# Fewer VectorE instructions and 640 side columns on DMA engines 0 to 4, in a decode layer with attention and a gated feed-forward

## The chip, the cores and the metric

The kernel runs on one core of a Trainium2 chip. The time of a run is device microseconds of that core. The span, which the profile shows, goes from the core's first to its last instruction and is about 2 us shorter than the time.

Names: PE is TensorE, DVE is VectorE, ACT is ScalarE, POOL is GpSimd, SP is SyncE. "DMA engine n" is one of the core's 16 DMA engines. A DMA over 128 rows (SBUF partitions) makes 128 packets in these traces and ends with 16 increments, so each DMA engine is taken to carry 8 rows. A completion increment is the step of a DMA's semaphore when one of its DMA engines has delivered its share. What waits for the load waits for the last increment (w1 before: last increment at 98.76 us, PE starts on it at 98.80). A traced instruction is one that the profile records, the waits included.

## The reference, cut to what matters

```python
# B = 4, D = 1024, Hq = 32, Hkv = 4, Dh = 128, F = 3584; one new token, the last 2048 cached keys
q = layernorm(x) @ wq                                  # wq: 1024 x 4096
o = softmax(q k^T / sqrt(128)) v                       # k, v: 4 batches x 4 heads x 2048 x 128
h = x + o @ wo                                         # wo: 4096 x 1024
n = layernorm(h)
out = h + (silu(n @ w1) * (n @ w3)) @ w2               # w1, w3: 1024 x 3584, w2: 3584 x 1024
```

All of it is bf16. The core reads 55.6 MB of weights and cache for four tokens.

## The kernel before

One SyncE queue streams the weights and the cache through a ring in SBUF, in a fixed order; each load waits only until its place in the ring is free.

```python
    CE = 512
    SETS = [(0, 5, 4), (80, 3, 4)]               # first row, DMA engines, tiles

    def load_side(r0, ne, ns):                   # some rows of wq's last CE columns
        t = ktpool.tile([P, JG * QD * 16], BF16, tag="kT")
        rows = A_wq[r0 * KC : (r0 + ne * 4 * ns) * KC, N_Q - CE : N_Q]
        rows = rows.rearrange("(t i k) n -> k i t n", i=ne, k=KC)[KC - 1]
        nc.sync.dma_start(out=t[: ne * 4, : ns * CE], in_=rows)
        return [t[: ne * 4, k * CE : (k + 1) * CE] for k in range(ns)]

    def load_tail(at, src, n, r0, m):            # the other half of wq, without those columns
        t = ring[:, at : at + m * n]
        nc.sync.dma_start(out=t[:, : m * n - CE], in_=src[:, r0 * n : (r0 + m) * n - CE])
        # ... cut
    plan = [
        ("wq", load_rows, (0, wq_v, N_Q, 0, 4)),
        ("side", load_side, SETS[0]),
        ("side", load_side, SETS[1]),
        ("wq", load_tail, (32 * KIB, wq_v, N_Q, 4, 4)),
        # ... k, v, wo, w1, w3 (cut)
        ("w2", load_rows, (56 * KIB, w2_v, D, 0, 17)),
        ("w2", load_rows, (90 * KIB, w2_v, D, 17, 7)),
        ("w2", load_rows, (104 * KIB, w2_v, D, 24, 3)),
        ("w2", load_rows, (110 * KIB, w2_v, D, 27, 1)),
    ]
```

The side loads are a balancing trick. Each of the 128 rows of wq's second half is loaded without its last 512 columns, which takes 8 KB off every DMA engine. These 128 pieces come in two extra DMAs shaped so that only a few DMA engines serve them: 80 pieces on DMA engines 0 to 4 (16 each) and 48 on 0 to 2 (16 each). PE multiplies them apart.

K is transposed by PE in 16 units of 16 blocks; each unit's result is copied from PSUM half by DVE and half by ACT, and the scores of a unit follow one unit later.

```python
    for u, (b, n) in enumerate(units):
        # ... k_v and kT (cut)
        for t in range(NJ // TB):                          # two halves of 8 blocks
            kt_ps = psA.tile([P, TB, P], BF16, tag=f"kt{nt % 4}")
            # ... 8 transposes (cut)
            if nt % 2 == 0:
                nc.vector.tensor_copy(out=kT[:, t * TB : (t + 1) * TB, :], in_=kt_ps[:])
            else:
                nc.scalar.copy(out=kT[:, t * TB : (t + 1) * TB, :], in_=kt_ps[:])
            nt += 1
        if u >= 1:
            emit_scores(u - 1)
        # ... cut
```

## Time and profile before

| | before |
|---|---|
| time, median (range) | 137.80 us (137.72 to 137.94, 6 runs) |
| span of the profiled run | 136.0 us |
| busy: PE, DVE, ACT, POOL | 72.3, 43.9, 31.0, 1.7 us |
| moved | 55.75 MB, mean 410 GB/s |
| w1 issued, landed | 76.27, 98.76 us |
| last w2 load landed | 132.68 us |

These lines are from the page of the kernel before: busy time by engine, the DMA share in 40 slices (tenths), what was moved, the DMA queues (packets, MB, share of 16 engines' span), and the chain of work that ended last, by engine.

```profile
span 136.0 us, 2436 instructions
...
PE 72.3 (53%) x1096; PEld 46.1 (34%) x1096; DVE 43.9 (32%) x79; ACT 31.0 (23%) x36; POOL 1.7 (1%) x8
...
DMA  5999999999999999999989999989989899999970
...
DMA packets 2650, 55.75 MB, mean 410 GB/s; under 512 B 296, under 2 KB 464, under 8 KB 720
...
q1 hardware_dynamic: 2604, 55.58, 95.6%
q8 instruction: 8, 0.13, 0.3%
...
q14 instruction: 2, 0.02, 0.0%
...
DMA 54%; PE 25%; ACT 11%; DVE 5%; SPq 2%; issue 1%; ACTq 0%
```

DMA stands at 8 or 9 tenths almost throughout, while no compute engine is over 53% busy. Two queues carry instructions: q8 brought eight packets, q14 two. They look negligible, at 0.3% and 0.0%.

The chain in order of time (start, us, what) shows that most of its last 60 us is waiting for landings; "ring<-in_B_w_dram" is the loads of w1, w3 and w2, L459 the w1 matmuls, L514 the last cast.

```profile
74.79 1.46 PE OT_ps L382 x48
...
76.27 22.49 DMA ring<-in_B_w_dram
...
98.80 1.68 PE g_ps L459 x14
100.48 29.74 DMA ring<-in_B_w_dram
...
133.08 0.27 ACT res L514
```

The two groups of DVE instructions that the change touches most (busy us and mean ns after the first bar, idle time before them after the second), and two waits (us in total, times, longest):

```profile
L323 DVE COPY kT<-kt_ps 128x1024 bf16<-128x1024 bf16 x16 | 11.1, 692 | 16.5 <-PE kt_ps L319 16.5
...
L356 DVE TENSOR_SCALAR z<-pt_ps,mask 128x512 bf16<-128x512 f32 x8 | 5.5, 741 | 1.2 <-ACT z L360 0.8 <-PE pt_ps L352 0.3
```

```profile
PE g_ps L459 <- DMA ring<-in_B_w_dram: 4.9, 1, 4.9
...
PE scores_ps L304 <- ACT kT L325: 2.9, 7, 0.6
```

PE waits 4.9 us for w1. This is the slack of the compute work between w1's issue and its landing. The issue of w1 has a slack of its own: the queue is still busy with wo, whose increments come from 80.02 to 81.87 us.

The single packets, read from the trace's record of them, give the time that one packet takes on its DMA engine:

```
bytes            512   1024   1280   2048   16384   31744   32768   57344   65536
median us      0.027  0.046  0.055  0.084   0.611   1.175   1.215   2.116   2.418
(1280: from the kernel after; 8 ns and about 27 GB/s fit all of them)
```

These are the 16 completion increments of the last w2 load (one row of w2 per partition), in us:

```
before  130.94 131.20 131.37 131.56 | 132.24 132.30 132.43 132.49 132.53 132.54 132.57 132.57 132.58 132.63 132.63 132.68
```

Four DMA engines are done about 1.2 us before the other twelve. What follows the last one is short; the timeline's last rows (start, us, engine, line, what) are the last matmul, the cast and the store:

```profile
132.79 0.23 PE L492 MATMUL yb_ps<-ring,hgT 128*32 128x128 bf16 x4
...
133.08 0.27 ACT L514 CAST res<-yb_ps 128x128 bf16<-128x128 f32 x1 [26.10 <-PE yb_ps L492]
133.39 0.64 ACTq L515 DMA_DIRECT2D out_dram<-res  x1
```

### The profile page before, as it was taken

How to read it: one execution, taken by the hardware profiler on the slowest of the kernel's cores; microseconds unless marked ns; L12 is line 12 of the kernel's file. 1: busy time of each engine (PE TensorE's matmuls, PEld its weight loads, DVE VectorE, ACT ScalarE, POOL GpSimd, SP SyncE). 2: the span in 40 equal slices, each digit the busy share in tenths (PEclk: the TensorE clock that was granted, in tenths of full speed). 3: DMA queues.
4: the chain of work that ended last, by engine and by line, in shares of the span. 5: the costliest groups of instructions: out<-in, count | busy, mean ns of one | idle time of the engine just before them, and what ended most of it. 6: DMA issues, size and time to landing. Idle time of an engine off the chain costs nothing.

```text
span 136.0 us, 2436 instructions
## 1 busy us (share of the span) xinstructions
PE 72.3 (53%) x1096; PEld 46.1 (34%) x1096; DVE 43.9 (32%) x79; ACT 31.0 (23%) x36; POOL 1.7 (1%) x8
## 2 busy tenths in 40 slices
PE   0004920979898989810525916791097000970981
PEld 0002300268374756500014905570043000430870
DVE  5055000043344444470994001206200596026010
ACT  3000000015555555609294300000001400000000
POOL 5000000000000000000000000000000000000000
PEclk9999975557999999985555555568556855568568
DMA  5999999999999999999989999989989899999970
GB/s 155 464 463 406 412 420 414 429 424 439 424 439 424 424 443 426 410 552 453 463 347 463 463 410 405 477 354 494 439 371 494 371 472 401 399 420 407 424 298 5
DMA packets 2650, 55.75 MB, mean 410 GB/s; under 512 B 296, under 2 KB 464, under 8 KB 720
## 3 DMA queue, kind: packets, MB, share of 16 engines
q1 hardware_dynamic: 2604, 55.58, 95.6%
q8 instruction: 8, 0.13, 0.3%
q10 hardware_dynamic: 36, 0.02, 0.0%
q14 instruction: 2, 0.02, 0.0%
HBM read 55.59 MB, written 0.01 MB: 409 GB/s over the span
## 4 chain that ended last, share of the span: by engine, by line
DMA 54%; PE 25%; ACT 11%; DVE 5%; SPq 2%; issue 1%; ACTq 0%
DMA ring<-in_B_w_dram 38%; DMA ring<-in_A_wq_dram 15%; PE kt_ps L319 11%; ACT kT L325 5%; PE scores_ps L304 5%; ACT z L360 3%; PE q_ps L263 3%; DVE rmax L336 2%; ACT Pm L341 2%; PE OT_ps L382 2%; DVE pT L350 1%; SPq L120 1%; PE g_ps L459 1%; DVE z L356 1%; ACT L341 1%
## 5 line engine op out<-in xcount | busy, mean ns | idle before, releaser
L325 ACT COPY kT<-kt_ps 128x1024 bf16<-128x1024 bf16 x16 | 15.9, 1013 | 13.4 <-PE kt_ps L319 13.4
L319 PE MATMUL kt_ps<-ident,ring 128*128 128x128 bf16 x256 | 18.0, 232 | 0.0
L319 PEld LDWEIGHTS <-ring 128*128 128x128 bf16 x256 | 16.0, 105 | 4.9 <-issue 4.9
L323 DVE COPY kT<-kt_ps 128x1024 bf16<-128x1024 bf16 x16 | 11.1, 692 | 16.5 <-PE kt_ps L319 16.5
L459 PEld LDWEIGHTS <-hnT 128*32 128x32 bf16 x128 | 5.5, 143 | 21.8 <-issue 19.2
L382 PE MATMUL OT_ps<-z,ring 128*128 128x32 bf16 x256 | 7.5, 188 | 8.5 <-ACT z L360 5.0
L459 PE MATMUL u_ps<-ring,hnT 128*32 128x448 bf16 x64 | 6.0, 563 | 11.0 <-DMA ring<-in_B_w_dram 11.0
L304 PE MATMUL scores_ps<-kT,qz 128*32 128x512 bf16 x64 | 9.9, 609 | 2.9 <-ACT kT L325 2.9
L263 PE MATMUL q_ps<-ring,xnT 128*4 128x512 bf16 x63 | 6.7, 595 | 7.8 <-DMA ring<-in_A_wq_dram 7.8
L382 PEld LDWEIGHTS <-ring 128*128 128x128 bf16 x256 | 7.4, 104 | 9.2 <-issue 9.2
L459 PE MATMUL g_ps<-ring,hnT 128*32 128x448 bf16 x64 | 5.9, 558 | 4.9 <-DMA ring<-in_B_w_dram 4.9
L492 PEld LDWEIGHTS <-hgT 128*32 128x32 bf16 x156 | 4.9, 134 | 6.2 <-issue 5.7
L411 PE MATMUL y_ps<-ring,o 128*32 128x256 bf16 x128 | 5.9, 371 | 0.8 <-DVE o L398 0.8
L514 ACT CAST res<-yb_ps 128x128 bf16<-128x128 f32 x1 | 0.3, 266 | 26.1 <-PE yb_ps L492 26.1
L492 PE MATMUL y_ps<-ring,hgT 128*32 128x256 bf16 x68 | 3.8, 419 | 4.4 <-DMA ring<-in_B_w_dram 4.4
L360 ACT ACTIVATE z<-pt_ps,mask 128x512 bf16<-128x512 f32 x8 | 5.3, 687 | 3.5 <-DVE z L356 3.5
L352 PE MATMUL pt_ps<-pT,perm 128*128 128x512 bf16 x4 | 2.4, 607 | 6.8 <-DVE pT L350 6.8
L263 PEld LDWEIGHTS <-xnT 128*4 128x4 bf16 x63 | 2.0, 115 | 11.7 <-issue 11.6
L194 PE MATMUL tp_ps<-ident,xn 4*128 4x4 bf16 x8 | 0.7, 200 | 10.0 <-DVE xn L187 10.0
L356 DVE TENSOR_SCALAR z<-pt_ps,mask 128x512 bf16<-128x512 f32 x8 | 5.5, 741 | 1.2 <-ACT z L360 0.8
L473 DVE RECIPROCAL eg<-eg 128x896 f32<-128x896 f32 x1 | 5.8, 5753 | 0.0
L411 PEld LDWEIGHTS <-o 128*32 128x32 bf16 x128 | 4.4, 131 | 3.1 <-DVE o L398 1.9
(85 smaller groups left out, 50.1 us busy)
## 6 DMA issues: line engine op xcount, KB each, us to landing
ring<-in_B_w_dram SPq DMA_DIRECT2D x2, 7168.0 KB, 22.5
ring<-in_A_k_cache_dram SPq DMA_DIRECT2D x4, 2048.0 KB, 27.6
ring<-in_A_v_cache_dram SPq DMA_DIRECT2D x4, 2048.0 KB, 29.2
ring<-in_B_w_dram SPq DMA_DIRECT2D x1, 4352.0 KB
ring<-in_A_wq_dram SPq DMA_DIRECT2D x1, 4096.0 KB, 12.2
ring<-in_A_wq_dram SPq DMA_DIRECT2D x1, 3968.0 KB
ring<-in_B_w_dram SPq DMA_DIRECT2D x1, 1792.0 KB
ring<-in_B_w_dram SPq DMA_DIRECT2D x1, 768.0 KB
```

The lines of the kernel that those rows point to most:

```text
L263: nc.tensor.matmul(q_ps[QD * g : QD * g + B, hf * 512 : hf * 512 + n], lhsT=xnT[:, kc, :], rhs=wq_t[:, c0 : c0 + n], start=(kc == 0), stop ...
L304: nc.tensor.matmul(scores_ps[QD * g : QD * (g + 1), n * 512 : (n + 1) * 512], lhsT=qz_v[:, z0 : z0 + QD], rhs=kT_v[:, g, :, :], start=(b = ...
L319: nc.tensor.transpose(out=kt_ps[:, jj, :], in_=k_v[:, n * NJ + t * TB + jj, :], identity=ident[:])
L323: nc.vector.tensor_copy(out=kT[:, t * TB : (t + 1) * TB, :], in_=kt_ps[:])
L325: nc.scalar.copy(out=kT[:, t * TB : (t + 1) * TB, :], in_=kt_ps[:])
L356: nc.vector.tensor_scalar(out=z[:, :, g, :], in0=pt_ps[:], scalar1=mask[:, g : g + 1], scalar2=None, op0=ALU.mult)
L360: nc.scalar.mul(out=z[:, :, g, :], in_=pt_ps[:], mul=mask[:, g : g + 1])
L382: nc.tensor.matmul(OT_ps[:, b, :], lhsT=loaded["v"][b][:, j, :], rhs=PTz[j // NJ][:, (j % NJ) * B + b, :, :], start=(j == 0), stop=(j == J ...
L411: nc.tensor.matmul(y_ps[QD * j : QD * (j + 1), :], lhsT=o4[:, i, :, :].rearrange("p b s -> p (b s)"), rhs=loaded["wo"][i][:, j * CG : (j + ...
L459: nc.tensor.matmul(out_ps[QD * j : QD * (j + 1), hf, :HF], lhsT=hnT[:, k, :], rhs=loaded[kind][k][:, c0 : c0 + HF], start=(k == 0), stop=( ...
L473: nc.vector.reciprocal(out=eg[:], in_=eg[:])
L492: nc.tensor.matmul(out_ps[QD * j : QD * (j + 1), :n], lhsT=hgT[:, i, :], rhs=loaded["w2"][i][:, j * CG + c0 : j * CG + c0 + n], **kw,)
```

## The change

The intent is fewer VectorE instructions and a better balance of the DMA engines. DVE copies whole K units (every other unit) and ACT the rest; scores follow two units later; softmax and norm operations are joined; setup moves to GpSimd. The side columns grow from 512 to 640, all their rows on DMA engines 0 to 4, and the side tiles move into the ring.

```diff
-    CE = 512
-    SETS = [(0, 5, 4), (80, 3, 4)]
+    CE = 640
+    SETS = [(0, 5, 6), (120, 2, 1)]
     ...
-        t = ktpool.tile([P, JG * QD * 16], BF16, tag="kT")
+        t = ring[:, at : at + ns * CE]
     ...
-        ("side", load_side, SETS[0]),
-        ("side", load_side, SETS[1]),
+        ("side", load_side, (144 * KIB, *SETS[0])),
+        ("side", load_side, (152 * KIB, *SETS[1])),
     ...
-    nc.vector.memset(eps_t[:], eps)
+    nc.gpsimd.memset(eps_t[:], eps)
     ... (x_q, qz, ident_f, perm and the side copies xs likewise; the table `same` is
          made by two DVE operations instead of seven)
+                for c0, c1 in ((CQ - CE, 512), (512, CQ)):       # each side tile in two matmuls
     ...
+        nj = NJ if u % 2 == 0 else TB
     ...
-            if nt % 2 == 0:
+            if u % 2 == 0 or (u == len(units) - 1 and j0 > 0):
-                nc.vector.tensor_copy(out=kT[:, t * TB : (t + 1) * TB, :], in_=kt_ps[:])
+                nc.vector.tensor_copy(out=kT[:, j0 : j0 + nj, :], in_=kt_ps[:])
     ...
-        if u >= 1:
-            emit_scores(u - 1)
+        if u >= 2:
+            emit_scores(u - 2)
     ...
-    nc.vector.reduce_max(out=rmax[:], in_=scores_ps[:], axis=AX.X)
-    nc.vector.tensor_single_scalar(out=nmax[:], in_=rmax[:], scalar=-1.0, op=ALU.mult)
+    nc.vector.reduce_max(out=nmax[:], in_=scores_ps[:], axis=AX.X, negate=True)
     ... (two mask multiplies by DVE become one tensor_tensor over both; norm 2 joins two pairs)
```

More of the change, by code (lines that the diff above doesn't have):

```diff
@@ L109, with load_side @@
     N_Q, N_F = Hq * Dh, F
-    CE = 512
-    SETS = [(0, 5, 4), (80, 3, 4)]
-    def load_side(r0, ne, ns):
-        t = ktpool.tile([P, JG * QD * 16], BF16, tag="kT")
+    CE = 640
+    SETS = [(0, 5, 6), (120, 2, 1)]
+    def load_side(at, r0, ne, ns):
+        t = ring[:, at : at + ns * CE]
         rows = A_wq[r0 * KC : (r0 + ne * 4 * ns) * KC, N_Q - CE : N_Q]
@@ L158 @@
         nc.scalar.dma_start(out=x_sb[:, c * 512 : (c + 1) * 512], in_=x_flat[:, c * 512 : (c + 1) * 512])
-    load_next(7)
+    load_next(6)
     ident = const.tile([P, P], BF16)
@@ L163 @@
     eps_t = const.tile([P, 1], FP32)
-    nc.vector.memset(eps_t[:], eps)
+    nc.gpsimd.memset(eps_t[:], eps)
     x_q = act.tile([P, CG], BF16)
-    nc.vector.memset(x_q[:], 0.0)
+    nc.gpsimd.memset(x_q[:], 0.0)
     for c in range(2):
@@ L191 @@
     xn_v = xn[:].rearrange("b (p kc) -> b kc p", kc=KC)
-    tp_ps = psA.tile([P, KC, B], BF16, tag="kt0")
+    tp_ps = psA.tile([P, KC, B], BF16, tag="k2")
     for kc in range(KC):
@@ L199 @@
     NS = sum(ns for _, _, ns in SETS)
-    ts_ps = psA.tile([P, NS, B], BF16, tag="kt1")
+    ts_ps = psA.tile([P, NS, B], BF16, tag="k3")
     xs = wide.tile([B, NS, 20], BF16, tag="w4k")
+    xsT = act.tile([20, NS, B], BF16)
     sl = []
@@ L205 @@
         v = v.rearrange("b (s l i k) -> b k l i s", s=4, l=ns, i=ne)
-        nc.vector.tensor_copy(
-            out=xs[:, len(sl) : len(sl) + ns, : ne * 4].rearrange("b l (i s) -> b l i s", s=4),
-            in_=v[:, KC - 1, :, :, :],
+        k0 = len(sl)
+        nc.gpsimd.tensor_copy(
+            out=xs[:, k0 : k0 + ns, : ne * 4].rearrange("b l (i s) -> b l i s", s=4), in_=v[:, KC - 1, :, :, :]
         )
@@ L211 @@
             nc.tensor.transpose(
-                out=ts_ps[: ne * 4, len(sl), :], in_=xs[:, len(sl), : ne * 4], identity=ident[:B, :B]
+                out=ts_ps[: ne * 4, k0 + l, :], in_=xs[:, k0 + l, : ne * 4], identity=ident[:B, :B]
             )
             sl.append(ne * 4)
-    xsT = act.tile([20, NS, B], BF16)
-    k0 = 0
-    for _, ne, ns in SETS:
         nc.vector.tensor_copy(out=xsT[: ne * 4, k0 : k0 + ns, :], in_=ts_ps[: ne * 4, k0 : k0 + ns, :])
-        k0 += ns
     q_ps = psA.tile([P, CQ], FP32, tag="scores")
@@ L225 @@
     qz = act.tile([P, B, Hkv * QD + REP], BF16)
-    nc.vector.memset(qz[:], 0.0)
+    nc.gpsimd.memset(qz[:], 0.0)
     ident_f = const.tile([P, P], FP32)
-    nc.vector.tensor_copy(out=ident_f[:], in_=ident[:])
+    nc.gpsimd.tensor_copy(out=ident_f[:], in_=ident[:])
     perm = const.tile([P, P], BF16)
-    nc.vector.tensor_copy(
+    nc.gpsimd.tensor_copy(
         out=perm[:].rearrange("p (h dq) -> p h dq", dq=JG),
@@ L244 @@
     same = const.tile([P, JG, QD], FP32)
-    nc.vector.tensor_tensor(out=same[:, 0, :], in0=ident[:, 0:QD], in1=ident[:, QD : 2 * QD], op=ALU.add)
-    for j in range(2, JG):
-        nc.vector.tensor_tensor(
-            out=same[:, 0, :], in0=same[:, 0, :], in1=ident[:, j * QD : (j + 1) * QD], op=ALU.add
-        )
-    nc.vector.tensor_single_scalar(out=same[:, 0, :], in_=same[:, 0, :], scalar=1.0 / JG, op=ALU.mult)
-    for j in range(1, JG):
-        nc.vector.tensor_copy(out=same[:, j, :], in_=same[:, 0, :])
+    fold = const.tile([P, QD], FP32)
+    nc.vector.reduce_sum(out=fold[:], in_=ident[:].rearrange("p (j x) -> p x j", j=JG), axis=AX.X)
+    nc.vector.tensor_single_scalar(
+        out=same[:], in_=fold[:].unsqueeze(1).to_broadcast([P, JG, QD]), scalar=1.0 / JG, op=ALU.mult
+    )
     for kc in range(KC):
@@ L267 @@
                     start=(kc == 0),
-                    stop=(kc == KC - 1 or (kc == KC - 2 and c0 + 512 == N_Q)),
+                    stop=(kc == KC - 1),
+                    skip_group_check=(g == JG - 1),
                 )
         if kc == RQ - 1:
-            load_next()
             for k, np_ in enumerate(sl):
-                nc.tensor.matmul(
-                    q_ps[QD * (JG - 1) : QD * (JG - 1) + B, CQ - CE : CQ],
-                    lhsT=xsT[:np_, k, :],
-                    rhs=loaded["side"][k],
-                    start=False,
-                    stop=False,
-                )
+                for c0, c1 in ((CQ - CE, 512), (512, CQ)):
+                    nc.tensor.matmul(
+                        q_ps[QD * (JG - 1) : QD * (JG - 1) + B, c0:c1],
+                        lhsT=xsT[:np_, k, :],
+                        rhs=loaded["side"][k][:, c0 - CQ + CE : c1 - CQ + CE],
+                        start=False,
+                        stop=False,
+                        skip_group_check=True,
+                    )
+            load_next(2)
     q_sb = act.tile([P, CQ], BF16)
@@ L282 @@
     nc.scalar.mul(out=q_sb[:, 512:], in_=q_ps[:, 512:], mul=qscale)
-    qt_ps = psA.tile([P, REP, P], BF16, tag="kt1")
+    qt_ps = psA.tile([P, REP, P], BF16, tag="k3")
     for r in range(REP):
@@ L310, in emit_scores @@
             )
-    nt = 0
     for u, (b, n) in enumerate(units):
@@ L315 @@
         kT = ktpool.tile([P, NJ, P], BF16, tag="kT")
-        for t in range(NJ // TB):
-            kt_ps = psA.tile([P, TB, P], BF16, tag=f"kt{nt % 4}")
-            for jj in range(TB):
+        nj = NJ if u % 2 == 0 else TB
+        for j0 in range(0, NJ, nj):
+            kt_ps = psA.tile([P, nj, P], BF16, tag="k01" if u % 2 == 0 else f"k{2 + j0 // TB}")
+            for jj in range(nj):
                 nc.tensor.transpose(
-                    out=kt_ps[:, jj, :], in_=k_v[:, n * NJ + t * TB + jj, :], identity=ident[:]
+                    out=kt_ps[:, jj, :], in_=k_v[:, n * NJ + j0 + jj, :], identity=ident[:]
                 )
-            if nt % 2 == 0:
-                nc.vector.tensor_copy(out=kT[:, t * TB : (t + 1) * TB, :], in_=kt_ps[:])
-            else:
-                nc.scalar.copy(out=kT[:, t * TB : (t + 1) * TB, :], in_=kt_ps[:])
-            nt += 1
+            if u % 2 == 0 or (u == len(units) - 1 and j0 > 0):
+                nc.vector.tensor_copy(out=kT[:, j0 : j0 + nj, :], in_=kt_ps[:])
+            else:
+                nc.scalar.copy(out=kT[:, j0 : j0 + nj, :], in_=kt_ps[:])
         kT_tiles.append(kT)
-        if u >= 1:
-            emit_scores(u - 1)
+        if u >= 2:
+            emit_scores(u - 2)
         if u == NSB * BS - 1:
             load_next()
+    emit_scores(len(units) - 2)
     emit_scores(len(units) - 1)
-    rmax = act.tile([P, 1], FP32)
-    nc.vector.reduce_max(out=rmax[:], in_=scores_ps[:], axis=AX.X)
     nmax = act.tile([P, 1], FP32)
-    nc.vector.tensor_single_scalar(out=nmax[:], in_=rmax[:], scalar=-1.0, op=ALU.mult)
+    nc.vector.reduce_max(out=nmax[:], in_=scores_ps[:], axis=AX.X, negate=True)
     Pm = wide.tile([P, W], BF16, tag="w4k")
@@ L348 @@
     PTz = []
+    pt2_ps = psA.tile([P, 2, NJ * B, REP], FP32, tag="k01")
     for c in range(NSB):
         nc.vector.transpose(out=pT[:, c, :], in_=Pm[:, c * 512 : (c + 1) * 512])
-        pt_ps = psA.tile([P, NJ * B, REP], FP32, tag=f"kt{c % 4}")
-        nc.tensor.matmul(pt_ps[:], lhsT=perm[:], rhs=pT[:, c, :], start=True, stop=True)
-        z = ktpool.tile([P, NJ * B, Hkv, REP], BF16, tag="kT")
-        for g in range(Hkv):
-            if g % 2 == 0:
-                nc.vector.tensor_scalar(
-                    out=z[:, :, g, :], in0=pt_ps[:], scalar1=mask[:, g : g + 1], scalar2=None, op0=ALU.mult
-                )
-            else:
-                nc.scalar.mul(out=z[:, :, g, :], in_=pt_ps[:], mul=mask[:, g : g + 1])
+        if c % 3 == 0:
+            pt_ps = pt2_ps[:, c // 3, :, :]
+        else:
+            pt1_ps = psA.tile([P, NJ * B, REP], FP32, tag=f"k{1 + c}")
+            pt_ps = pt1_ps[:]
+        nc.tensor.matmul(pt_ps, lhsT=perm[:], rhs=pT[:, c, :], start=True, stop=True)
+        z = ktpool.tile([P, NJ * B, Hkv, REP], BF16, tag="kT")
+        nc.vector.tensor_tensor(
+            out=z[:, :, 0:Hkv:2, :],
+            in0=pt_ps.unsqueeze(2).to_broadcast([P, NJ * B, 2, REP]),
+            in1=mask[:, 0:Hkv:2].unsqueeze(1).unsqueeze(3).to_broadcast([P, NJ * B, 2, REP]),
+            op=ALU.mult,
+        )
+        for g in range(1, Hkv, 2):
+            nc.scalar.mul(out=z[:, :, g, :], in_=pt_ps, mul=mask[:, g : g + 1])
         PTz.append(z)
@@ L370 @@
     )
-    bc_ps = psA.tile([P, B, Hq], FP32, tag="kt2")
+    bc_ps = psA.tile([P, B, Hq], FP32, tag="k2")
     nc.tensor.matmul(
@@ L376 @@
     nc.scalar.copy(out=bc[:], in_=bc_ps[:])
-    OT_ps = psA.tile([P, B, Hq], FP32, tag="kt1")
+    OT_ps = psA.tile([P, B, Hq], FP32, tag="scores")
     for b in range(B):
@@ L395 @@
     nc.vector.transpose(out=oT[:].rearrange("p b i -> p (b i)"), in_=OT_sb[:].rearrange("p b h -> p (b h)"))
-    o4_ps = psA.tile([P, B, IO], FP32, tag="kt3")
+    o4_ps = psA.tile([P, B, IO], FP32, tag="k3")
     nc.tensor.matmul(o4_ps[:], lhsT=perm[:], rhs=oT[:], start=True, stop=True)
@@ L428 @@
     nc.vector.bn_aggr(out=mv2[:], in_=st2[:])
-    msq = act.tile([P, 1], FP32)
-    nc.vector.tensor_tensor(out=msq[:], in0=mv2[:, 0:1], in1=mv2[:, 0:1], op=ALU.mult)
-    nc.vector.tensor_tensor(out=mv2[:, 1:2], in0=mv2[:, 1:2], in1=msq[:], op=ALU.add)
+    nc.vector.scalar_tensor_tensor(
+        out=mv2[:, 1:2], in0=mv2[:, 0:1], scalar=mv2[:, 0:1], in1=mv2[:, 1:2], op0=ALU.mult, op1=ALU.add
+    )
     sums_ps = psB.tile([P, 2], FP32, tag="sums")
@@ L435 @@
     nc.vector.tensor_copy(out=tot[:], in_=sums_ps[:])
-    nc.vector.tensor_tensor(out=msq[:], in0=tot[:, 0:1], in1=tot[:, 0:1], op=ALU.mult)
-    var = act.tile([P, 1], FP32)
-    nc.vector.tensor_tensor(out=var[:], in0=tot[:, 1:2], in1=msq[:], op=ALU.subtract)
+    nvar = act.tile([P, 1], FP32)
+    nc.vector.scalar_tensor_tensor(
+        out=nvar[:], in0=tot[:, 0:1], scalar=tot[:, 0:1], in1=tot[:, 1:2], op0=ALU.mult, op1=ALU.subtract
+    )
     rstd2 = act.tile([P, 1], FP32)
-    nc.scalar.activation(out=rstd2[:], in_=var[:], func=ACT.Sqrt, bias=eps_t[:], scale=1.0)
+    nc.scalar.activation(out=rstd2[:], in_=nvar[:], func=ACT.Sqrt, bias=eps_t[:], scale=-1.0)
     nc.vector.reciprocal(out=rstd2[:], in_=rstd2[:])
```

## The prediction

> **What bounds it.** The DMA stream. The page's DMA slices read 8 or 9 nearly throughout; 55.75 MB move at 410 GB/s. Packet by packet, 16 KB takes 0.611 us and 57 KB 2.116 us on an engine (27 GB/s), the next starting as the last ends. No engine idles from 1.8 us to its end at 131 to 132.7, except about 0.9 us where it serves one of eight 16 KB instruction fetches. The chain of waits agrees: its last 60 us are landings (22.5 us to w1, 29.7 us to w2).
>
> VectorE is 32% busy. It matters only through the issue of w1 (at 76.27 us), gated by the PV matmuls of batch 1. The queue holds wo until 80.0 (first engine) to 81.9 us, so attention has 2 to 3 us of slack, and finishing it earlier buys nothing.
>
> **What the change does.**
> - K copies: 16 DVE copies of 692 ns and 16 ACT copies of 1013 ns become 8 DVE copies of twice the size (estimate 1.3 us), one of the old, and 15 ACT copies. Scores lag two units, so PE stops waiting for ACT (2.9 us in all): attention 2 to 3 us earlier. Off path.
> - Softmax: the 153 ns negation goes; 8 DVE multiplies (741 ns) become 4 (estimate 1.1 to 1.3 us). Off path.
> - Norm 2: two 159 ns operations go; its result is ready at 96.2 us, before w1 lands at 98.76. Off path.
> - Setup: PE waits for wq until 23.66 us anyway. Off path.
> - Batch 1's V tile waits for the side matmuls (ended near 17.9 us); the queue holds K until 43 us. No gap.
> - DMA bytes: the same. Side rows go from 128 to 160 KB, all on engines 0 to 4 (the Trainium skill, "DMA: Bandwidth & Descriptors", how many engines a DMA uses; the trace agrees: five and three completion increments for the two side loads). Every engine's wq tail shrinks by 8 x 256 B = 2 KB, 0.076 us at 27 GB/s.
>
> Is that 0.076 us on the path? The completion increments of the last w2 load fall in two groups: four at 130.94 to 131.56 us, twelve at 132.24 to 132.68. I read the late ones as the engines hit by a fetch (0.9 us, and a neighbouring packet stretched by about 0.55) plus engines 0 to 2, with 32 side packets of 46 ns (1.47 us). After: engines 0 and 1 carry 28 packets of an estimated 55 ns (1.54 us, less 0.076: unchanged), engine 2 fewer; 3 and 4 use spare time; fetched engines gain 0.076 us. The last landing moves 0 to 0.08 us earlier.
>
> **Prediction: 137.7 us, 80% range 137.3 to 138.0.** Faster by over 2%: 0.02; within 2%: 0.95; slower by over 2%: 0.03.
>
> **Right if** DVE busy falls from 43.9 to 38 to 41 us, w1 issues at 71 to 76 us, the DMA row has no new gap, w1 still lands near 98.7 and the last w2 row at 132.5 to 132.7, with the tail (3.3 us) unchanged. **A step is wrong** if w1's landing moves with its issue, or the late group loses members.
>
> **What would make it wrong:** a drop of the granted clock (0.5 from 59.9 us on) coming earlier and holding the K stage beyond the slack; a fetch moving to engines 0 to 4, adding up to 1.4 us at the end; or an added fetch, as PE has ten more instructions.

## The result, and the profile after

| | before | after |
|---|---|---|
| time, median (range) | 137.80 us (137.72 to 137.94, 6 runs) | 138.50 us (138.34 to 138.91, 6 runs) |
| span, profiled run | 136.0 us | 136.4 us |
| busy: PE, DVE, ACT, POOL | 72.3, 43.9, 31.0, 1.7 us | 74.0, 41.8, 29.2, 3.7 us |
| w1 issued, landed | 76.27, 98.76 us | 71.85, 99.27 us |
| last w2 load landed | 132.68 us | 133.10 us |
| time less span, mean | 1.82 us | 2.06 us |

The ratio is 1.0055, 95% interval 1.004 to 1.0071. A ratio here is the mean time of one kernel's runs over that of the other's of the same rounds, so it is not quite the ratio of the medians. Executions over 1.5% slower than the fastest of the same kernel are left out of the means. The change is within 2%, but it is clearly slower, by 0.7 us, and outside the range that was forecast. "Time less span" is the mean over the runs, each run's time less its own span, which is listed to 0.1 us (for before, over the nine runs of it that stood beside the first experiments; their mean span is 136.02 us, and 136.06 us in the two later sessions).

The same lines of the page of the kernel after:

```profile
span 136.4 us, 2413 instructions
...
PE 74.0 (54%) x1101; PEld 46.5 (34%) x1101; DVE 41.8 (31%) x53; ACT 29.2 (21%) x35; POOL 3.7 (3%) x15
...
DMA  5999998999999999999999798998989989998960
...
DMA packets 2648, 55.74 MB, mean 409 GB/s; under 512 B 295, under 2 KB 463, under 8 KB 719
...
q1 hardware_dynamic: 2603, 55.58, 95.3%
q8 instruction: 8, 0.13, 0.3%
...
q14 instruction: 1, 0.01, 0.0%
...
DMA 58%; PE 24%; ACT 8%; DVE 5%; SPq 2%; issue 1%; ACTq 0%
```

The chain in order of time, the two DVE groups and the waits:

```profile
70.38 1.46 PE OT_ps L383 x48
...
71.85 27.41 DMA ring<-in_B_w_dram
...
99.31 2.41 PE g_ps L461 x19
...
101.85 31.25 DMA ring<-in_B_w_dram
...
133.48 0.27 ACT res L516
```

```profile
L320 DVE COPY kT<-kt_ps 128x2048 bf16<-128x2048 bf16 x8 | 9.8, 1225 | 15.8 <-PE kt_ps L316 15.8
...
L354 DVE TENSOR_TENSOR z<-pt_ps,mask 128x1024 bf16<-128x1024 f32 x4 | 4.7, 1205 | 0.4 <-ACT z L361 0.4
```

```profile
PE g_ps L461 <- DMA ring<-in_B_w_dram: 9.4, 1, 9.4
...
PE y_ps L412 <- DMA ring<-in_A_wo_dram: 4.2, 1, 4.2
...
PE scores_ps L301 <- ACT kT L322: 1.2, 2, 0.6
```

Most of the compute part came as foreseen. DVE has fewer instructions (its busy time, 41.8 us, misses the foreseen 38 to 41), PE's wait for ACT's copies before scores fell from 2.9 to 1.2 us, and w1 is issued 4.4 us earlier. PE then waits 9.4 us instead of 4.9 for it, and 4.2 us for wo: the gain turned into waiting. But w1 does not land at the same time; it lands 0.5 us later, and what is behind it, up to the last w2 load and the store, comes 0.4 us later. (The 7 in the DMA row after is no gap. The row seems to count a packet with its whole time where it starts; packets laid out from start to end fill every slice from the 2nd to the 38th, before and after.)

```profile
133.19 0.24 PE L494 MATMUL yb_ps<-ring,hgT 128*32 128x128 bf16 x4
...
133.48 0.27 ACT L516 CAST res<-yb_ps 128x128 bf16<-128x128 f32 x1 [26.39 <-PE yb_ps L494]
133.79 0.64 ACTq L517 DMA_DIRECT2D out_dram<-res  x1
```

The increments of the w1 load, and of the last w2 load, show that this is one DMA engine alone:

```
w1 before   97.00  97.09  97.11  97.25  97.43  97.61 | 98.42  98.48  98.54  98.61  98.65  98.69  98.71  98.72  98.75  98.76
w1 after    96.70  96.93  96.93  97.03  97.22 | 98.05  98.22  98.31  98.36  98.44  98.46  98.52  98.58  98.59  98.59 | 99.27
w2 before  130.94 131.20 131.37 131.56 | 132.24 132.30 132.43 132.49 132.53 132.54 132.57 132.57 132.58 132.63 132.63 132.68
w2 after   130.64 130.86 131.04 131.16 | 132.00 132.14 132.15 132.19 132.29 132.31 132.31 132.41 132.47 132.52 132.53 | 133.10
```

Fifteen DMA engines end earlier than before, as the prediction had it, though by more: 0.1 to 0.4 us, compared rank by rank, where it had 0 to 0.08. One ends 0.57 us after all others. It fell behind between the landing of wo (last increment 81.73 us, nothing stands out there) and that of w1.

What happened in between? These are the instruction fetches by start time in us (16 KB on q8, eight of them for PE's 2,201 traced instructions; 8 KB on q14):

```
before  q8 32.00 43.73 54.55 79.61 86.06 92.61 105.23 130.63   q14 60.63 135.65
after   q8 27.17 43.51 53.68 72.28 79.72 88.06 105.05 130.66   q14 93.74
```

The DMA view of a 2 us window, 60 to 62 us before and 93 to 95 us after, shows the 8 KB fetch (packets, MB, share; packets count with their whole time where they start, so a share can pass 100%):

```profile
q1 hardware_dynamic: 43, 1.03, 121.4%
q14 instruction: 1, 0.01, 1.0%
```

```profile
q1 hardware_dynamic: 16, 0.92, 107.5%
q14 instruction: 1, 0.01, 1.0%
```

Each of these fetches is one packet in the trace, so one DMA engine serves it. Following single packets, a 16 KB fetch leaves a gap of 0.86 to 0.95 us on that DMA engine and stretches the packet beside it by 0.47 to 0.55 us, together 1.4 us. The 8 KB fetch leaves 0.30 and stretches by 0.53: 0.84 us.

The 8 KB fetch at 60.63 us before comes when DVE has started 59 traced instructions; the one at 93.74 us after, when it has started 61. ACT's traced count before is 65 when the one at 135.65 starts. In the experiments below DVE's comes at 61 to 66 started instructions and ACT's at 64 or 65. So these look like the fetch of the next block when DVE or ACT has passed some 60 traced instructions. The change did not remove DVE's fetch; it only came later, as DVE goes from 103 traced instructions to 74 (waits included).

### The profile page after: what moved, and what is told of

It reads as the page before. It is cut to its first block, busy times and chain, and to the rows that moved or that the text cites. A ratio compares the mean times of both kernels' runs of the same rounds, so it can differ in the third digit from the quotient of the medians.

```text
span 136.4 us, 2413 instructions
## 1 busy us (share of the span) xinstructions
PE 74.0 (54%) x1101; PEld 46.5 (34%) x1101; DVE 41.8 (31%) x53; ACT 29.2 (21%) x35; POOL 3.7 (3%) x15
## 4 chain that ended last, share of the span: by engine, by line
DMA 58%; PE 24%; ACT 8%; DVE 5%; SPq 2%; issue 1%; ACTq 0%
DMA ring<-in_B_w_dram 43%; DMA ring<-in_A_wq_dram 15%; PE kt_ps L316 12%; PE scores_ps L301 6%; ACT z L361 4%; ACT kT L322 3%; PE q_ps L257 3%; PE g_ps L461 2%; DVE z L354 2%; DVE nmax L333 2%; ACT Pm L336 2%; DVE pT L346 1%; SPq L120 1%; PE OT_ps L383 1%; PE qt_ps L282 1%
## 5 line engine op out<-in xcount | busy, mean ns | idle before, releaser
L322 ACT COPY kT<-kt_ps 128x1024 bf16<-128x1024 bf16 x15 | 14.5, 1014 | 13.1 <-PE kt_ps L316 13.1
L320 DVE COPY kT<-kt_ps 128x2048 bf16<-128x2048 bf16 (+1 forms) x9 | 10.5, 1166 | 16.2 <-PE kt_ps L316 16.2
L257 PE MATMUL q_ps<-ring,xnT 128*4 128x512 bf16 (+1 forms) x63 | 7.2, 625 | 3.4 <-DMA ring<-in_A_wq_dram 3.4
L412 PEld LDWEIGHTS <-o 128*32 128x32 bf16 x128 | 5.2, 136 | 6.0 <-issue 5.3
L474 DVE TENSOR_SCALAR eg<-eg 128x896 f32<-128x896 f32 x1 | 0.6, 627 | 15.2 <-ACT eg L473 15.2
L354 DVE TENSOR_TENSOR z<-pt_ps,mask 128x1024 bf16<-128x1024 f32 x4 | 4.7, 1205 | 0.4 <-ACT z L361 0.4
```

What stands on the lines that cost most here:

```text
L257: nc.tensor.matmul(q_ps[QD * g : QD * g + B, hf * 512 : hf * 512 + n], lhsT=xnT[:, kc, :], rhs=wq_t[:, c0 : c0 + n], start=(kc == 0), stop ...
L320: nc.vector.tensor_copy(out=kT[:, j0 : j0 + nj, :], in_=kt_ps[:])
L322: nc.scalar.copy(out=kT[:, j0 : j0 + nj, :], in_=kt_ps[:])
L354: nc.vector.tensor_tensor(out=z[:, :, 0:Hkv:2, :], in0=pt_ps.unsqueeze(2).to_broadcast([P, NJ * B, 2, REP]), in1=mask[:, 0:Hkv:2].unsqueez ...
L412: nc.tensor.matmul(y_ps[QD * j : QD * (j + 1), :], lhsT=o4[:, i, :, :].rearrange("p b s -> p (b s)"), rhs=loaded["wo"][i][:, j * CG : (j + ...
```

## The experiments

Theory A: DVE's 8 KB fetch falls on DMA engine 3 or 4. Before, these two carried 16 side packets (0.74 us, half of what 0 to 2 carried), so the 0.84 us fitted into their spare time. The change gave them 24 packets of 55 ns (1.32 us), and now the sum shows. Rival B: a PE fetch falls on a DMA engine that was already late, because PE has more instructions or runs earlier. Rival C: it is not the stream at all but something outside the span. Ten kernels were run, all with correct results.

### e1: the changed kernel with the old side rows

```diff
-    CE = 640
-    SETS = [(0, 5, 6), (120, 2, 1)]
+    CE = 512
+    SETS = [(0, 5, 4), (80, 3, 4)]
-                for c0, c1 in ((CQ - CE, 512), (512, CQ)):
+                for c0, c1 in ((512, 768), (768, CQ)) if k < 6 else ((512, CQ),):
```

> The changed kernel with the side rows of the kernel before (512 columns; 32 packets on engines 0 to 2, 16 on engines 3 and 4) and the same number of PE instructions. Theory A (the 8 KB VectorE instruction fetch falls on engine 3 or 4, and the change raised that engine's side load from 16 packets of 46 ns to 24 of 55 ns, so its 0.59 us comes on top): the single late increment of the last w2 load disappears, the last landing goes from 133.10 to about 132.6 us, time about 0.5 us below the changed kernel (near 138.0). Rival B (a PE instruction fetch hits an engine already late, because PE has more instructions or earlier ones): the late one stays, time 138.5. Rival C (nothing in the stream, only overhead outside the span): time 138.5.

Measured: 138.10 us (before on the same chip 137.80; ratio 1.0017, interval 1.0004 to 1.003). The late one is gone; the last w2 load ends 132.49 132.50 132.55 132.57 132.60 132.62 132.65 132.65, as in the kernel before. The mean span is 136.02 us, equal to that of before. The end of its timeline, its last matmul and its store:

```profile
132.88 0.23 PE L494 MATMUL yb_ps<-ring,hgT 128*32 128x128 bf16 x4
...
133.47 0.64 ACTq L517 DMA_DIRECT2D out_dram<-res  x1
```

So the side rows are needed for the 0.4 to 0.5 us in the span. The rest of the change, with w1 issued at 72.19 instead of 76.27 us, moves the span by nothing. The time is still 0.3 us above before, and that lies outside the span (time less span 2.06 us, against 1.82). Rival C is right about that part alone.

### e2: the kernel before with the new side rows

```diff
-    CE = 512
-    SETS = [(0, 5, 4), (80, 3, 4)]
+    CE = 640
+    SETS = [(0, 5, 3), (60, 5, 3), (120, 2, 1)]
... (a third side load in the plan; side matmuls in two parts, as in the changed kernel)
```

> The kernel before with the change's side rows alone (640 columns, 24 packets of 1280 B on engines 0 to 4 and 4 more on 0 and 1; three loads instead of two because its buffers are smaller). Theory A: one engine of the last load lands about 0.5 us after the others, near 133.1 us, time 138.2 to 138.4. Rivals B and C: time 137.8, as the instruction streams are those of before.

Measured: 138.27 us (ratio 1.0033, interval 1.0021 to 1.0046). One DMA engine is late again: 132.56 132.66 132.72, then 133.05. The mean span is 136.52 us, the same as the changed kernel's.

```profile
133.15 0.24 PE L496 MATMUL yb_ps<-ring,hgT 128*32 128x128 bf16 x4
...
133.75 0.63 ACTq L519 DMA_DIRECT2D out_dram<-res  x1
```

DVE is not shortened here, and its 8 KB fetch comes at 59.91 us. Following the packets, that fetch falls on a DMA engine with 24 side packets. This following goes from the end of one packet to the start that fits best, and can confuse two DMA engines that end within some ns of each other; in this run the counts of side packets come out whole (28, 28, 24, 24, 24 on five of them), but it cannot tell safely which of them ends last, some 70 us later.

The increments tell that without following. These are the last four of the load before DVE's fetch, and of the next one, in the three kernels with a late one:

```
e2     fetch  59.91    57.36  57.54  57.63  57.69    62.37  62.52  62.53 | 63.02
after  fetch  93.74    81.67  81.68  81.69  81.73    98.58  98.59  98.59 | 99.27
e4     fetch 117.76   115.55 115.56 115.64 115.75   125.85 125.90 126.01 | 126.75
```

Three fetches at three different times, and each time the next load is the first with a late one. In e2 and e4 (told below) no PE fetch starts between the two loads, which speaks against rival B; in the changed kernel one does, at 88.06 us.

### e3: the changed kernel without DVE's fetch

```diff
-    nc.vector.tensor_copy(out=xnT[:], in_=tp_ps[:])
+    nc.scalar.copy(out=xnT[:], in_=tp_ps[:])
... (xsT, qz and o4 copies and the last K copy to ScalarE; fold, same, Dm and the
     addition of 1 before the reciprocal to GpSimd; four transposes of P as two)
```

> The changed kernel with 15 fewer VectorE instructions (moved to ScalarE and GpSimd, two transposes joined), few enough that VectorE should need no second 8 KB instruction fetch while the stream runs; side rows as changed. Theory A: no 8 KB fetch between 0 and 130 us, all late increments within 0.6 us, last landing about 132.5 us, time about 0.6 us below the changed kernel (near 137.9). Rival B: the late increment stays, 138.5. Rival C: 138.5 unless the ScalarE count matters.

Measured: 138.02 us (ratio 1.0009, interval 0.9996 to 1.0022), mean span 136.00 us. DVE has 59 traced instructions, and the DMA view up to 134 us has no q14 line:

```profile
q1 hardware_dynamic: 2603, 55.58, 97.0%
q8 instruction: 8, 0.13, 0.3%
q10 hardware_dynamic: 16, 0.01, 0.0%
```

The last increments are 132.46 132.53 132.67 132.76. The single late one is gone although the side rows are the new ones and PE's eight fetches are all there, so rival B falls. With this the square is closed: old rows with the fetch (before, e1) and new rows without it (e3) have no late one, new rows with it (the changed kernel, e2) have one. The group as a whole did not get as early as expected (132.76 us, not 132.5); why is open.

### e4 and e10: which DMA engine

e4 puts all 128 side rows, 512 columns, on DMA engines 0 to 3; e10 puts them, 384 columns, on 0 to 2.

```diff
e4:  +    CE = 512;  SETS = [(0, 4, 8)]
e10: +    CE = 384;  SETS = [(0, 3, 10), (120, 2, 1)]
```

> The changed kernel with all 128 side rows (512 columns) on engines 0 to 3, 32 packets of 46 ns (1.47 us) each, none on engine 4. Theory A with the VectorE fetch on engine 4: no late one, last landing about 132.6, time near 138.0. Theory A with it on engine 3 or lower: late one 0.1 to 0.2 us later than in the changed kernel, last landing about 133.2, time 138.6. Rivals B and C: as the changed kernel.

> The changed kernel with the 128 side rows on engines 0 to 2 only (384 columns, 40 to 44 packets of an estimated 36 ns, 1.45 to 1.6 us), so engines 3 and 4 carry none. If the 8 KB VectorE fetch falls on engine 3 (e4, which still loaded engine 3, had the late increment; the kernel before had none with 0 to 2 loaded more than 3): no single late increment, last landing 132.6 to 132.8 us, time minus span as in the changed kernel, time 138.1. If it falls on engine 2 or lower: a late increment near 133.3, time 138.7.

Measured: e4 138.84 us (ratio 1.0075, interval 1.0061 to 1.0089), last increments 132.58 132.59 132.70, then 133.43: the late one is there, 0.33 us later than in the changed kernel, where 0.1 to 0.2 was expected (the sum of 32 x 46 ns less 24 x 55 ns, and 0.076 us for the longer wq tail, gives 0.23). Its fetch, at 117.76 us, is seen in the DMA view of 117 to 119 us:

```profile
q1 hardware_dynamic: 25, 0.87, 102.3%
q14 instruction: 1, 0.01, 1.0%
```

e10: 138.20 us (ratio 1.0024, interval 1.0012 to 1.0036), last increments 132.69 132.73 132.74 132.80: none stands out, although DVE's fetch is there at 92.93 us. Loading 0 to 3 collides and loading 0 to 2 doesn't, so DVE's fetch falls on DMA engine 3, if it falls on the same one in all these kernels. The trace does not number the DMA engines, so this is an inference.

### The 0.25 us outside the span: e5 to e9

What happens after the last instruction of the span is called the exit here. The time less span is 1.78 to 1.84 us in the kernel before and in e2, and 2.05 to 2.06 in the changed kernel, e1, e4 and e10. Theory D: it hangs on how many instructions ACT executes. Rival: on GpSimd's longer stream.

e5 is e1 with 11 tiny ACT copies at the start. e6 is e1 with the setup work put back on DVE. e7 is e3 with 3 tiny ACT copies.

```diff
e5:  +    for i in range(11):
     +        nc.scalar.copy(out=pad_a[:, i : i + 1], in_=pad_z[:])
e6:  -    nc.gpsimd.memset(eps_t[:], eps)
     +    nc.vector.memset(eps_t[:], eps)
     ... (x_q, xs, qz, ident_f, perm likewise)
```

> What is open: 0.25 us that the time has and the span has not (time minus span is 1.79 us before and with the old kernel plus new side rows, 2.0 to 2.1 us in the changed kernel and with old side rows). Theory D: it hangs on ScalarE's instruction count: in the kernel before ScalarE has 66 traced instructions and its second 8 KB instruction fetch comes at 135.65 us, inside the span, while the output store is under way; the changed kernel has 54 and no such fetch. This kernel is e1 (old side rows) with 11 tiny ScalarE copies at the start, so the count is that of before. D: time minus span falls to about 1.8 us, time near 137.8. Rival E (it hangs on GpSimd's work or anything else of the change): time minus span stays at 2.05, time 138.1.

> e1 (old side rows) with the setup work put back from GpSimd to VectorE, so that GpSimd has as many instructions as before; ScalarE stays at about 54. Theory D: time minus span stays near 2.05 us, time 138.1. Rival E with GpSimd as the cause: time minus span near 1.8, time 137.8.

> The version that both theories point to: the changed kernel with 15 fewer VectorE instructions (as e3, no 8 KB VectorE fetch in the stream) and ScalarE padded to the count of before. Theories A and D: last w2 landing about 132.6 us, time minus span about 1.8, time 137.7, equal to before within 0.15 us. If D is wrong: 138.0 as e3.

Measured: e5 137.90 us (ratio 0.9999, interval 0.9987 to 1.0012), time less span 1.85: as theory D has it. But e6 also came down, 137.79 us (ratio 0.9992, interval 0.9978 to 1.0006), time less span 1.78, which theory D had not expected; and e7 stayed up, 138.13 us (ratio 1.0017, interval 1.0004 to 1.003), 2.11. e7's miss has a visible partner: an 8 KB fetch at 137.88 us, after its span, and e3 has two, at 137.11 and 137.93 us. In e7 DVE has 59 traced instructions, about the count at which it fetches. e6 differs from e1 in GpSimd's count, and by one instruction in ACT's (53 instead of 54). So the theory was narrowed (D2): the cost comes when an engine ends a few instructions short of the count, so that the fetch falls into the exit. Two kernels set it against GpSimd:

```diff
e8 (e6 and):  +        nc.scalar.copy(out=pad_a[:, i : i + 1], in_=eps_t[:])      # twice
e9 (e6 and):  +        nc.gpsimd.memset(pad_p[:, i : i + 1], 0.0)                 # 8 times
```

> e6 (old side rows, setup on VectorE) with two or three more ScalarE instructions, so that ScalarE has one or two more than in the changed kernel while GpSimd has as many as before. Theory D2 (the 0.25 us outside the span comes when ScalarE has 58 or so instructions and crosses the next instruction boundary in the exit): time minus span rises from 1.78 to about 2.05 us, time 138.05. Theory G (it comes from GpSimd's longer stream): time minus span stays near 1.78, time 137.8.

> e6 with 8 tiny GpSimd memsets (0.1 us each) at the start, so that GpSimd has as many instructions as in the changed kernel, and ScalarE stays at e6's count. Theory G: time minus span rises to about 2.05 us, time 138.05. Theory D2: it stays near 1.78, time 137.8.

Measured: e8 138.07 us (ratio 1.0014, interval 1.0002 to 1.0026), time less span 2.00. e9 137.93 us (ratio 0.9998, interval 0.9985 to 1.0011), 1.79. GpSimd's count does nothing, ACT's does:

| kernel | ACT traced | DVE traced | GpSimd traced | time less span, us |
|---|---|---|---|---|
| before | 66 | 103 | 23 | 1.82 |
| e2 | 67 | 106 | 23 | 1.78 |
| e5 | 66 | 74 | 31 | 1.85 |
| e6 | 53 | 79 | 23 | 1.78 |
| e9 | 53 | 79 | 31 | 1.79 |
| after | 54 | 74 | 30 | 2.06 |
| e1 | 54 | 74 | 30 | 2.06 |
| e8 | 56 | 79 | 23 | 2.00 |
| e3 | 62 | 59 | 36 | 1.97 |
| e7 | 66 | 59 | 37 | 2.11 |

ACT counts of 54 and 56 cost about 0.2 us; 53, 66 and 67 do not, but for e7. e3 and e7 have DVE at 59, so e3 does not tell what an ACT count of 62 costs, and e7, with ACT at 66, points to DVE; no run varies DVE's count alone. That ACT's count matters is shown in both directions: 12 more ACT instructions remove the cost (e1 to e5), three more bring it (e6 to e8), while GpSimd's count (e9) does nothing. That the way is a fetch in the exit is seen only in e3 and e7, whose traces reach that far; in the changed kernel's trace no such fetch is recorded, so there it stays an inference.

No kernel beat the one before beyond its interval; e3, e5, e6 and e9 cannot be told from it.

## Why the prediction was right or wrong

- What bounds the kernel: right. The span did not move when w1 was issued 4 us earlier (e1: mean span 136.02 us, as before).
- The compute side: right in direction, off the critical path. DVE busy 41.8 us was above the foreseen 38 to 41, because two overlapping setup operations were slow (the multiply that makes `same` took 1.58 us, one 8x4 copy of xsT 1.27 us). Both ran while GpSimd did the setup work that was moved to it. In e6 and e9, where that work is back on DVE, the same multiply takes 0.23 us and DVE is busy for 41.6 us: moving the setup saved DVE no busy time. The double K copy, at 1225 ns, came out a little below the 1.3 us that was foreseen.
- The landing of fifteen DMA engines: right in direction only. They end 0.1 to 0.4 us earlier than before, where 0 to 0.08 was forecast; why is open.
- The step that failed is "3 and 4 use spare time". One of the two (engine 3, by e10's inference) had none: a fetch of 8 KB by DVE, 0.84 us, already filled it. So the overlap was wrong, and with it the forecast that the last landing moves 0 to 0.08 us earlier; it moved 0.42 us later. The prediction counted eight 16 KB fetches and overlooked the 8 KB one at 60.63 us in the same record, although the twelve late increments need it: three DMA engines with 32 side packets and eight PE fetches, on one DMA engine each, make eleven. (The w1 load before shows the same sum: ten late ones after six PE fetches.) The term is the side load of that DMA engine: 24 x 55 ns less 16 x 46 ns is 0.58 us, less the 0.076 us of the shorter wq tail is 0.51 us; measured, the last landing moved from 132.68 to 133.10 us in the profiled runs and the mean span by 0.50 us. e2 shows it by adding the side rows alone, e1 by removing them, e3 by removing the fetch.
- The prediction warned of a fetch moving to DMA engines 0 to 4. It had not moved to another DMA engine, as far as e10's inference holds; it was there before.
- "With the tail unchanged" was right within the span (3.3 us from the last landing to the end) and missed what lies outside it. ACT went from 66 to 54 instructions and the time less span from 1.82 to 2.06 us. The two terms, 0.50 and 0.24 us, make the 0.7 us of the medians. The prediction had no term for this.

## What to carry to other kernels

When the DMA stream is the bound, as here, the kernel ends with its slowest DMA engine: read all 16 completion increments of the last load, not only the mean rate, before giving one DMA engine more. Count every client of a DMA engine, instruction fetches of each compute engine among them; together with the side rows, a queue with a share of 0.0% moved this kernel by 0.5 us. Removing instructions off the critical path can still cost time (here 0.2 us in the exit). When work is moved to another engine, look at what the first one's remaining operations then take (`same`: 1.58 us beside GpSimd's work, 0.23 us without it).

## What the Trainium skill lacked or had wrong

- "Runtime: NRT & Kernel Launch", section "Instruction fetch mechanics", says that an engine's instructions are refilled in 16 KiB blocks of 256 instructions. That agrees for PE (eight 16 KB fetches, some 2,200 instructions); for DVE and ACT the fetches in these traces are 8 KB, and come when 59 to 66 traced instructions have started.
- The same section calls the cost of a block boundary mostly hidden. It counts no time of the DMA engines, and in this kernel, bound by DMA, that was not hidden: each 16 KB fetch took about 1.4 us from one DMA engine's stream (0.9 us of gap, 0.5 us of a stretched packet), and each 8 KB fetch 0.84 us.
- No page read says which DMA engine serves a fetch. "DMA: Bandwidth & Descriptors", section "Why a DMA increments its semaphore by 16 and not by 1", says that a load on fewer than 16 DMA engines takes the lowest-numbered ones, and e2's packet counts (28, 28, 24, 24, 24 on five DMA engines) agree with that. DVE's fetch was worked out to be on DMA engine 3, an inference from e4 and e10.
- No page read tells of the 0.2 us that this program pays in its exit when ACT ends at 54 or 56 traced instructions (2.06 and 2.00 us of time less span in e1 and e8, against 1.78 at 53 in e6 and 1.85 at 66 in e5).
